# Low halves of the values: a scaled Scalar copy and a GpSimd subtraction in place of one Vector operation with a running sum

## The chip, the cores and the metric

The kernel runs on one core of a Trainium2 chip. The metric is device microseconds of one launch, the median of the runs shown. Engines are named as in the profile: PE (TensorE matmul) and PEld (its weight loads), DVE (VectorE), ACT (ScalarE), POOL (GpSimd), SP (SyncE, which issues nearly all DMAs here).

## What is computed

Top-32 attention over 4 batches and 8 heads, then a dense two-layer block with squared ReLU, then a routed layer with 8 experts. Shapes: q, k, v are 4 x 8 x 576 x 64; the dense block is 512 to 2048 to 512.

```python
scores = scale * np.matmul(q, k.transpose(0, 1, 3, 2))
kth = np.partition(scores, -top_k, axis=-1)[..., -top_k:-top_k + 1]
scores = np.where(scores >= kth, scores, -1e9)
attn = softmax(scores)                    # rows of 576, 32 kept
attn_out = np.matmul(attn, v)             # -> x, 2304 tokens x 512
...
x = np.square(np.maximum(x @ w_in, 0)) @ w_out
...
# then by token: e = argmax(x @ w_gate); out = x + gate * relu(x @ w1[e]) @ w2[e]
```

## The kernel before

Every fp32 factor that goes into a matmul is held as two fp16 numbers, a high half (the value, scaled by a power of two and rounded to fp16) and a low half (the scaled value less the high half). Products are the sum of high x high, low x high and high x low.

**The attention part** is a loop over 72 ticks `j`. A tick takes two score tiles of 128 queries x 576 keys (`a`, `b`). PE makes the scores of the next tick's tiles (`qk`, line 326), ACT copies them out of PSUM (`evac_s`, line 332), and DVE finds the 32nd largest score of each row: `tree` (line 360) takes the larger and the smaller of each pair of scores, `top32` runs four rounds of MAX8 (line 379) with MATCH_REPLACE8 between (line 382), and `mask` (line 406) compares the scores with the 32nd. ACT takes the exponential (line 401), POOL multiplies it by the mask (line 415), ACT makes the high half of the weights and their row sum (line 430), POOL the low half (line 435), and an SP DMA transposes both into `pt` (line 437). Three ticks later (`AV_LAG`) PE multiplies `pt` by the values (`av`, line 458). `e` has 3 buffers, `phl` 3, `pt` 7.

**Loads and halves of q, k and v** are "pieces". `fetch(j)` issues a piece's load into the ring `raw` of 3 buffers (line 201, an SP DMA), up to two ticks ahead; `prep(j)` makes the halves, at most three pieces a tick by its planner. For q (lines 220 to 222) and k (lines 227 to 231) ACT writes the high half, ACT scales `raw` in place, and POOL subtracts; the subtraction is put on the list `low_pool`, which is run in the middle of the next tick. For v there are 32 pieces of 128 x 320 (two heads of four pairs in four batches): ACT writes the high half into `vh[:, :, 0:D]` (line 242) and a DVE operation on the list `low_dve` makes the low half (line 245). That operation scales `raw`, subtracts the high half, writes fp16 and also sums its results along the row into one column of `v_low`; in the trace the sum is read out by a second row, DVE_READ_ACCUMULATOR. `low_dve` is run behind `top32` and ahead of the next `tree`.

**Beside the attention** run, in ticks up to 7, the conversion of the dense weights (ACT lines 278, 284, 303; DVE lines 291, 293; POOL line 304), and from tick 8 the dense block on finished tokens: PE lines 535 and 568, ACT lines 543 to 547, POOL line 556 (`gh`, the low half of the squared ReLU). After the loop come routing and the experts.

**Order.** The instructions are recorded in the order of the code and a scheduler that plans ahead with a timeline then sets the order on each engine; `tc.issue_after` keeps an instruction behind a named one. So an engine's order can change wherever a piece of work changes.

**The checks.** Near the end 128 x n tables of bounds are compared with limits (`check`, lines 1170 to 1176); if any fails, a plain path computes everything again. `v_low` is one of these tables (lines 1188 to 1190).

Of the kernel before, what the change touches and what calls it, by code (L numbers as in the profile page):

```python
# [9 lines left out]
F32 = mybir.dt.float32  # L10
# [5 lines left out]
AF = mybir.ActivationFunctionType  # L16
ALU = mybir.AluOpType
AX = mybir.AxisListType
# [3 lines left out]
B, H, S, D = 4, 8, 576, 64  # L22
# [7 lines left out]
V_EXP, W_EXP, R_EXP = 12, 8, 12  # L30
# [69 lines left out]
def attention_two_moes(ctx, tc, qm, qc, kd, vd, w_in, w_out, w_g, w1, w2, cst, out):  # L100
    nc = tc.nc
    const = ctx.enter_context(tc.tile_pool(name="const", bufs=1))
# [17 lines left out]
    nc.vector.memset(ones, 1.0)  # L120
    wgs = const.tile([128, 4, 9], F32, name="wgs")
    lg_all = const.tile([128, NT, 9], F32, name="lg_all")
    v_low = const.tile([128, 4 * H], F32, name="v_low")
    w_sq = const.tile([128, 20], F32, name="w_sq")
    w_abs = const.tile([128, 32], F32, name="w_abs")
    x_sq = const.tile([128, NT + 4], F32, name="x_sq")
# [77 lines left out]
    def new_k():  # L204
        return apool.tile([128, S], F16, name="kh", bufs=2 * BUFS["k"])

    def new_v():
        return apool.tile([128, 5, 2 * D], F16, name="vh", bufs=BUFS["v"])

    low_pool, low_dve = [], []  # L210

    def prep_piece(pc):
        vi, kind, hd, t = pc["vi"], pc["kind"], pc["hd"], pc["raw"]
        v_ = visits[vi]
        if kind[0] == "q":
            n = {"qm": 512, "ql": 256, "qc": 192}[kind]
            q = apool.tile([128, 2, n], F16, name=kind, tag=kind if kind == "qc" else "qm", bufs=BUFS[kind])
            if kind == "ql":
                t = t.rearrange("p h t -> p (h t)")
            nc.scalar.activation(q[:, 0], t, AF.Copy, scale=2.0 ** QK_EXP)  # L220
            nc.scalar.activation(t, t, AF.Copy, scale=2.0 ** QK_EXP)
            low_pool.append(lambda: nc.gpsimd.tensor_sub(q[:, 1], t, q[:, 0]))
            vq[vi, kind[:2] if kind == "qc" else "qm"] = q
        elif kind == "k":
            kh = [new_k() for _ in range(2)]
            h, l = (apool.tile([128, S], F16, name=n, bufs=2) for n in ("hp", "lp"))
            nc.scalar.activation(h, t, AF.Copy, scale=2.0 ** QK_EXP)
            nc.scalar.activation(t, t, AF.Copy, scale=2.0 ** QK_EXP)

            def finish():  # L230
                nc.gpsimd.tensor_sub(l, t, h)
                for hd in range(2):
                    for n, x in enumerate((h, l)):
                        nc.sync.dma_start(kh[hd][64 * n:64 * n + 64], x[64 * hd:64 * hd + 64])

            low_pool.append(finish)
            for hd in range(2):
                vq["k", v_["b"], v_["pr"], hd] = kh[hd]
        else:
            vh = new_v()  # L240
            t3 = t.rearrange("p (c d) -> p c d", c=5)
            nc.scalar.activation(vh[:, :, 0:D], t3, AF.Copy, scale=2.0 ** V_EXP)
            vq["v", v_["b"], v_["pr"], hd] = vh
            slot = (v_["b"] * 4 + v_["pr"]) * 2 + hd
            low_dve.append(lambda: nc.vector.scalar_tensor_tensor(
                out=vh[:, :, D:], in0=t3, scalar=2.0 ** V_EXP, in1=vh[:, :, 0:D],
                op0=ALU.mult, op1=ALU.subtract, accum_out=v_low[:, slot:slot + 1]))

    def run_all(jobs):
        while jobs:  # L250
# [86 lines left out]
    def scores(a):  # L337
        with tc.high_priority():
            qk(a)
            qk(a + 1)  # L340
            evac_s(a)
# [75 lines left out]
    def rinv(a):  # L417
        l = st[a]["pair"][2]
        nc.vector.reciprocal(l[:, 1], l[:, 0])
# [233 lines left out]
    def conv(step, j, lo, hi):  # L653
        for it in conv_at.get(j, [])[lo:hi]:
            step(*it)
# [20 lines left out]
    for j in range(NJ + AV_LAG + 1):  # L676
        a, b = 2 * j, 2 * j + 1
        live = a < NTILE
        nxt = a + 2 < NTILE
        prev = 1 <= j <= NJ  # L680
        pa, pb = a - 2, b - 2
        back = [a - 2 * AV_LAG, b - 2 * AV_LAG] if AV_LAG <= j < NJ + AV_LAG else []
        tick[0] = j
        for c in GRAM.get(j, ()):
            gram(c)
        conv(conv_split, j - 1, 2, 4)
        conv(load_w64, j, 2, 4)
        if nxt:
            scores(a + 2)
        conv(conv_act, j, 0, 2)  # L690
        step_units(HALVES / 2)
        step_units(HALVES / 2)
        conv(conv_dve, j, 0, 2)
        if live:
            if j == 0:
                tree(a)
            pair_tiles(a)
            tail = top32(a, back)
            for job in low_dve:
                with tc.issue_after(tail):  # L700
                    tail = job().ins
            low_dve.clear()
            if nxt:
                with tc.issue_after(tail):
                    tail = tree(a + 2)
            with tc.issue_after(tail):
                mask(a)
                mask(b)
        elif back:
            rinv(back[0])  # L710
        if live:
            exp_s(a)
        conv(conv_split, j, 0, 2)
        conv(conv_act, j, 2, 4)
        conv(conv_dve, j, 2, 4)
        if prev:
            apply_mask(pa)
            apply_mask(pb)
        run_all(low_pool)
        g_low()  # L720
        fetch(j)
        conv(load_w64, j + 1, 0, 2)
        if prev:
            high(pa)
            high(pb)
        x_split()
        if prev:
            low(pa)
        if live:
            exp_s(b)  # L730
        if prev:
            low(pb)
            keep_bounds(pa)
        logits()
        for i in back:
            av(i)
        for i in back:
            xout(i)
        prep(j)
        logits_turn()  # L740
# [6 lines left out]
    rpool = ctx.enter_context(tc.tile_pool(name="route", bufs=1, side="right"))  # L747
# [418 lines left out]
    good = rpool.tile([128, 9], F32, name="good")  # L1166
# [3 lines left out]
    def check(n, x, limit, op):  # L1170
        t = test[:, :x.shape[1]]
        if isinstance(limit, float):
            nc.vector.tensor_scalar(out=t, in0=x, scalar1=limit, scalar2=None, op0=op)  # L1173
        else:
            nc.vector.tensor_tensor(out=t, in0=x, in1=limit, op=op)
        nc.vector.tensor_reduce(out=good[:, n:n + 1], in_=t, axis=AX.X, op=ALU.min)  # L1176

    m15, m23, m31 = (bounds[:, :, n] for n in range(3))
# [6 lines left out]
    check(4, w_sq, 2.0 ** 17.5, ALU.is_le)  # L1185
    check(5, w_sq, 512.0, ALU.is_ge)
    check(6, w_abs, 2.0 ** -97, ALU.is_le)
    vl = rpool.tile([128, 4 * H], F32, name="vl")
    nc.vector.tensor_tensor(out=vl, in0=v_low, in1=v_low, op=ALU.mult)
    check(7, vl, 9216.0 ** 2, ALU.is_le)  # L1190
    check(8, m31, 2.0 ** -6, ALU.is_ge)
    nc.vector.tensor_reduce(out=good[:, 8:9], in_=good[:, 0:9], axis=AX.X, op=ALU.min)
    cnt_f = rpool.tile([128, 8], F32, name="cnt_f")
    nc.vector.tensor_copy(cnt_f, cnt)
    nc.vector.tensor_reduce(out=cnt_max, in_=cnt_f, axis=AX.X, op=ALU.max)
# [215 lines left out]
```

## Time and profile before

| what | us |
|---|---|
| median of 3 runs (lowest, highest) | 1027.3 (1023.33, 1030.25) |
| the profiled execution, own time | 1023.65 |
| its span | 1021.8 |
| DVE busy | 845.7 (83%) |
| PE busy | 779.8 (76%) |
| POOL busy | 767.4 (75%) |
| ACT busy | 759.8 (74%) |

The profile is one execution. Between the first and the last instruction lie 1021.8 us; the own time is 1.85 us longer. A busy share over the whole span mixes stages: the attention loop fills the first 745 us, the experts the last 250, and each has its own limit. So the views below are read by stretch. A row of a group gives an operation's busy time and mean duration, and how long its engine sat idle just before it.

### The profile page before, as it was taken

How to read it: one execution, taken by the hardware profiler on the slowest of the kernel's cores; microseconds unless marked ns; L12 is line 12 of the kernel's file. 1: busy time of each engine (PE TensorE's matmuls, PEld its weight loads, DVE VectorE, ACT ScalarE, POOL GpSimd, SP SyncE). 2: the span in 40 equal slices, each digit the busy share in tenths (PEclk: the TensorE clock that was granted, in tenths of full speed). 3: DMA queues.
4: the chain of work that ended last, by engine and by line, in shares of the span. 5: the costliest groups of instructions: out<-in, count | busy, mean ns of one | idle time of the engine just before them, and what ended most of it. 6: DMA issues, size and time to landing. Idle time of an engine off the chain costs nothing. (4 is left out here: it accounts for less than half of the span.)

```text
span 1021.8 us, 25759 instructions
## 1 busy us (share of the span) xinstructions
PE 779.8 (76%) x9036; PEld 592.5 (58%) x9036; DVE 845.7 (83%) x2279; ACT 759.8 (74%) x2117; POOL 767.4 (75%) x783
## 2 busy tenths in 40 slices
PE   0123337989879979989969999999997958688852
PEld 0122226767667757667657777767775746565631
DVE  4999999999999999999989999999908634535631
ACT  7777676899988998888779989999866642544620
POOL 4576777899879898888879988899955875744850
PEclk9999999999999999999979999999998978898876
DMA  9675554668675475565475676565537508653500
GB/s 286 174 189 152 141 126 78 103 137 156 118 161 111 94 150 94 108 130 119 100 137 121 138 138 130 116 117 90 96 64 269 208 27 326 214 177 113 177 15 10
DMA packets 257023, 138.16 MB, mean 135 GB/s; under 512 B 215348, under 2 KB 238260, under 8 KB 256848
## 3 DMA queue, kind: packets, MB, share of 16 engines
q1 hardware_dynamic: 253568, 132.16, 55.7%
q0 software_dynamic: 3280, 3.80, 1.2%
q8 instruction: 94, 1.54, 0.6%
q14 instruction: 81, 0.66, 0.2%
HBM read 76.92 MB, written 7.37 MB: 82 GB/s over the span
## 5 line engine op out<-in xcount | busy, mean ns | idle before, releaser
L379 DVE MAX8 m<-tr 128x8 f32<-128x288 f32 (+1 forms) x576 | 275.8, 517 | 0.0
L435 POOL TENSOR_TENSOR phl<-e,phl 128x576 f16<-128x576 f32 x144 | 190.6, 1328 | 33.2 <-ACT phl L430 29.0
L415 POOL TENSOR_TENSOR e<-e,mk 128x576 f32<-128x576 f32 x144 | 196.0, 1371 | 21.9 <-DVE mk L406 21.9
L568 PE MATMUL px<-woh,gh 128*128 128x512 f16 x576 | 189.3, 382 | 15.9 <-POOL gh L556 10.8
L382 DVE MATCH_REPLACE8 tr<-m,tr 128x288 f32<-128x288 f32 x432 | 186.8, 437 | 0.0
L535 PEld LDWEIGHTS <-wih 128*128 128x128 f16 x2048 | 143.2, 101 | 55.4 <-issue 23.6
L535 PE MATMUL ph<-xb,wih 128*128 128x128 f16 (+1 forms) x1792 | 156.6, 231 | 21.0 <-DMA xb<-xhl 9.5
L458 PE MATMUL misc<-vh,pt 128*128 128x64 f16 (+1 forms) x2400 | 119.3, 198 | 63.7 <-ACT xn L476 33.7
L556 POOL TENSOR_TENSOR gh<-g,gh 128x128 f16<-128x128 f32 (+1 forms) x256 | 130.2, 515 | 41.1 <-ACT gh L547 27.4
L458 PEld LDWEIGHTS <-pt 128*128 128x128 f16 (+1 forms) x2400 | 100.8, 100 | 85.3 <-issue 53.2
L568 PEld LDWEIGHTS <-gh 128*128 128x128 f16 x864 | 77.5, 100 | 86.0 <-POOL gh L556 21.1
L360 DVE SCALAR_TENSOR_TENSOR tr<-pS,s 128x576 f32<-128x576 f32 x144 | 102.1, 750 | 14.8 <-ACT s L332 10.8
L401 ACT ACTIVATE e<-s,nm 128x576 f32<-128x576 f32 x144 | 111.0, 772 | 1.4 <-POOL phl L435 0.7
L568 PE MATMUL px<-wol,gh 128*128 128x512 f16 x288 | 109.7, 382 | 0.0
L430 ACT ACTIVATE phl<-e 128x577 f16<-128x577 f32 x144 | 98.0, 681 | 2.8 <-POOL e L415 2.8
L543 ACT ACTIVATE r<-ph 128x128 f32<-128x128 f32 (+1 forms) x256 | 70.3, 287 | 37.9 <-PE ph L535 36.8
L535 PE MATMUL ph<-xb,wil 128*128 128x128 f16 (+1 forms) x896 | 97.4, 230 | 0.0
L326 PE MATMUL pS<-kh,ql 128*128 128x192 f16 x576 | 67.2, 273 | 38.9 <-DMA kh<-lp 26.1
L406 DVE TENSOR_SCALAR mk<-s,m 128x576 f16<-128x576 f32 x144 | 93.3, 688 | 0.0
L545 ACT ACTIVATE g<-r 128x128 f32<-128x128 f32 (+1 forms) x256 | 82.7, 324 | 7.1 <-POOL gh L556 3.4
L332 ACT ACTIVATE s<-pS 128x1152 f32<-128x1152 f32 x72 | 80.3, 1116 | 3.7 <-PE pS L326 3.4
L547 ACT ACTIVATE gh<-r 128x128 f16<-128x128 f32 (+1 forms) x256 | 80.7, 320 | 1.3 <-PE px L568 1.0
(229 smaller groups left out, 1585.6 us busy)
## 6 DMA issues: line engine op xcount, KB each, us to landing
wraw<-in_w SPq DMA_DIRECT2D x64, 512.0 KB, 5.4
wol<-in_w_in SPq DMA_DIRECT2D x16, 512.0 KB, 4.9
raw<-in_qm SPq DMA_DIRECT2D x48, 128.0 KB, 2.8
w<-in_w_out SPq DMA_DIRECT2D x10, 512.0 KB, 3.7
raw<-in_vd SPq DMA_DIRECT2D x32, 160.0 KB, 2.8
raw<-in_kd SPq DMA_DIRECT2D x16, 288.0 KB, 3.5
out<-x SPq DMA_DIRECT2D x16, 256.0 KB, 2.6
wol<-in_w_out SPq DMA_DIRECT2D x6, 512.0 KB, 3.7
```

The source lines that it names most:

```text
L360: last = nc.vector.scalar_tensor_tensor(out=R2[:, :, n * 288:n * 288 + 288].rearrange("p k (c x) -> p k c x", c=3), in0=near, scalar=2.0 * ...
L379: return both(lambda k: nc.vector.max(m[k][:, 8 * r:8 * r + 8], x[k][:, :n]))
L382: both(lambda k: nc.vector.match_replace(out=dst[k][:, :n], in_to_replace=m[k][:, 8 * r:8 * r + 8], in_values=src[k][:, :n], imm_value=NEG))
L401: nc.scalar.activation(e[:, :S], st[i]["s"], AF.Exp, scale=0.125, bias=st[i]["nm"])
L406: nc.vector.tensor_scalar(out=t, in0=st[i]["s"], scalar1=st[i]["m"][:, 31:32], scalar2=None, op0=ALU.is_ge)
L415: nc.gpsimd.tensor_mul(e[:, :S], e[:, :S], st[i]["mk"])
L430: nc.scalar.activation(h[:, 0, :S + 1], st[i]["e"], AF.Copy, accum_out=st[i]["l"][:, 0:1])
L435: nc.gpsimd.tensor_sub(h[:, 1, :S], st[i]["e"][:, :S], h[:, 0, :S])
L458: nc.tensor.matmul(ps[:, a, :], lhsT=pt[:rows, 5 * low + c, :], rhs=vh[:rows, c, part * D:(part + 1) * D], start=(n == 0), stop=(n == len( ...
L535: nc.tensor.matmul(ph, lhsT=wt[:, d, u["f"] * 128:(u["f"] + 1) * 128], rhs=x[:, :, c0 + d, :], start=(n == 0), stop=(n == 11))
L556: g_last[0] = nc.gpsimd.tensor_sub(u["gh"][:, 1], u["g"], u["gh"][:, 0]).ins
L568: nc.tensor.matmul(px, lhsT=gh[:, part, t * 128:(t + 1) * 128], rhs=w[:, f, :], start=(f == 0 and n == 0), stop=(f == 15 and n == 2))
```

## The change

```diff
-    v_low = const.tile([128, 4 * H], F32, name="v_low")
...
-    low_pool, low_dve = [], []
+    low_pool = []
...
             nc.scalar.activation(vh[:, :, 0:D], t3, AF.Copy, scale=2.0 ** V_EXP)
             vq["v", v_["b"], v_["pr"], hd] = vh
-            slot = (v_["b"] * 4 + v_["pr"]) * 2 + hd
-            low_dve.append(lambda: nc.vector.scalar_tensor_tensor(
-                out=vh[:, :, D:], in0=t3, scalar=2.0 ** V_EXP, in1=vh[:, :, 0:D],
-                op0=ALU.mult, op1=ALU.subtract, accum_out=v_low[:, slot:slot + 1]))
+            nc.scalar.activation(t, t, AF.Copy, scale=2.0 ** V_EXP)
+            low_pool.append(lambda: nc.gpsimd.tensor_sub(vh[:, :, D:], t3, vh[:, :, 0:D]))
...
             tail = top32(a, back)
-            for job in low_dve:
-                with tc.issue_after(tail):
-                    tail = job().ins
-            low_dve.clear()
...
-    vl = rpool.tile([128, 4 * H], F32, name="vl")
-    nc.vector.tensor_tensor(out=vl, in0=v_low, in1=v_low, op=ALU.mult)
-    check(7, vl, 9216.0 ** 2, ALU.is_le)
-    check(8, m31, 2.0 ** -6, ALU.is_ge)
-    nc.vector.tensor_reduce(out=good[:, 8:9], in_=good[:, 0:9], axis=AX.X, op=ALU.min)
+    check(7, m31, 2.0 ** -6, ALU.is_ge)
+    nc.vector.tensor_reduce(out=good[:, 8:9], in_=good[:, 0:8], axis=AX.X, op=ALU.min)
```

The values now take the path of q and k: two ACT copies and a POOL subtraction. The sum, its table and its check are gone. In the changed kernel line numbers are lower by 1 to 3 in the loop (`tree` is L357 there, `mask` L403, the mask multiplication L412, the low half of the weights L432); the new rows are L243 on ACT and L244 on POOL.

The scheduler moves other rows too. Three places show what stands around the new and the removed rows. The first is DVE, in the third batch, one tick with a value piece. Before (`m_6519` is the 32 best of the tile pair):

```order
L379 MAX m_6519<-tr 128x8 x2
L419 RECIPROCAL l<-l 128x2
L382 MATCH_REPLACE tr<-m_6519,tr 128x288 x2
L379 MAX m_6519<-tr 128x8 x2
L245 SCALAR_TENSOR_TENSOR vh,v_low<-raw,vh 128x5x64
L360 SCALAR_TENSOR_TENSOR tr<-pS,s 128x2x288 x2
L406 TENSOR_SCALAR mk<-s,m_6519 128x576 x2
```

With the change, in the same batch:

```order
L376 MAX m_6534<-tr 128x8 x2
L416 RECIPROCAL l<-l 128x2
L379 MATCH_REPLACE tr<-m_6534,tr 128x288 x2
L376 MAX m_6534<-tr 128x8 x2
L357 SCALAR_TENSOR_TENSOR tr<-pS,s 128x2x288 x2
L403 TENSOR_SCALAR mk<-s,m_6534 128x576 x2
```

The value row between the last MAX and the next tree is gone; the rest of the tick's DVE chain stands in the same order.

The second place is ACT, in the same batch (`s` is the copy of the next scores, `nm` the row maximum for the exponential, `r`, `g`, `gh` the dense block). Before:

```order
L387 ACTIVATE nm<-m_6519 128x2
L332 ACTIVATE s<-pS 128x1152
L401 ACTIVATE e_94<-s,nm 128x576
L430 ACTIVATE phl_98,l<-e_92 128x577
L543 ACTIVATE r<-ph 128x128 x2
L430 ACTIVATE phl_99,l<-e_93 128x577
L242 ACTIVATE vh<-raw 128x5x64
L545 ACTIVATE g<-r 128x128
L547 ACTIVATE gh<-r 128x128
L476 ACTIVATE xn<-misc,l 128x64 x2
```

With the change:

```order
L384 ACTIVATE nm<-m_6534 128x2
L329 ACTIVATE s<-pS 128x1152
L398 ACTIVATE e_93<-s,nm 128x576
L540 ACTIVATE r<-ph 128x128
L241 ACTIVATE vh<-raw 128x5x64
L427 ACTIVATE phl_97,l<-e_91 128x577
L542 ACTIVATE g<-r 128x128
L544 ACTIVATE gh<-r 128x128
L243 ACTIVATE raw<-raw 128x320
L473 ACTIVATE xn<-misc,l 128x64 x2
```

The new scaling row stands a few rows behind the high half, both behind the copy of the scores and ahead of the next tick's.

The third place is POOL, in the same batch (`e` by mask, `phl` the low half of the weights, `lp` the low half of k). Before:

```order
L435 TENSOR_TENSOR phl_100<-e_94,phl_100 128x576
L231 TENSOR_TENSOR lp<-raw,hp 128x576
L435 TENSOR_TENSOR phl_98<-e_92,phl_98 128x576
L556 TENSOR_TENSOR gh<-g,gh 128x128 x2
L415 TENSOR_TENSOR e_93<-e_93,mk 128x576
L556 TENSOR_TENSOR gh<-g,gh 128x128
L415 TENSOR_TENSOR e_94<-e_94,mk 128x576
```

With the change, two value rows stand within one tick:

```order
L412 TENSOR_TENSOR e_91<-e_91,mk 128x576
L553 TENSOR_TENSOR gh<-g,gh 128x128
L244 TENSOR_TENSOR vh<-raw,vh 128x5x64
L432 TENSOR_TENSOR phl_99<-e_93,phl_99 128x576
L553 TENSOR_TENSOR gh<-g,gh 128x128
L432 TENSOR_TENSOR phl_97<-e_91,phl_97 128x576
L553 TENSOR_TENSOR gh<-g,gh 128x128
L244 TENSOR_TENSOR vh<-raw,vh 128x5x64
L553 TENSOR_TENSOR gh<-g,gh 128x128
L412 TENSOR_TENSOR e_92<-e_92,mk 128x576
```

Each value subtraction stands directly ahead of a low half of the weights or shortly ahead of a mask multiplication, in the one queue of POOL.

## Rows read from the trace of the kernel before

**Rows 1.** The page: span, and each engine's busy time over it.

```profile
span 1021.8 us, 25759 instructions
PE 779.8 (76%) x9036; PEld 592.5 (58%) x9036; DVE 845.7 (83%) x2279; ACT 759.8 (74%) x2117; POOL 767.4 (75%) x783
```

**Rows 2.** Stretches: us, PE, PEld, DVE, ACT, POOL busy (count), clock, DMA share, GB/s.

```profile
0.00:152.00 152.00, 37.75 (x319) 28.25 (x319) 136.02 (x277) 111.62 (x242) 100.95 (x85) 1.00 0.65 179
152.00:745.00 593.00, 536.69 (x6602) 412.63 (x6603) 578.52 (x1696) 520.32 (x1591) 513.37 (x562) 0.97 0.63 119
240.00:268.00 28.00, 25.53 (x316) 18.74 (x314) 27.79 (x83) 26.68 (x83) 26.42 (x32) 1.00 0.82 151
250.00:310.00 60.00, 51.40 (x660) 39.60 (x658) 59.79 (x176) 54.52 (x175) 51.51 (x59) 0.97 0.68 137
434.00:508.00 74.00, 68.54 (x670) 49.79 (x669) 72.74 (x206) 60.64 (x174) 61.35 (x61) 0.95 0.60 117
555.00:592.00 37.00, 36.96 (x422) 28.46 (x420) 36.58 (x108) 33.88 (x91) 35.12 (x37) 1.00 0.69 136
592.00:656.00 64.00, 59.31 (x789) 46.33 (x788) 63.54 (x185) 57.47 (x186) 52.84 (x61) 0.97 0.66 132
```

**Rows 3.** Waits of DVE, 75 to 760 us: waiter, releaser, us, times, longest.

```profile
DVE tr L360 <- ACT s L332: 5.1, 3, 3.4
DVE l L419 <- ACT phl L430: 3.8, 1, 3.8
DVE sq L518 <- PE ph L515: 1.2, 1, 1.2
```

**Rows 4.** Lines by source: count, shortest/median/longest ns, first and last start.

```profile
L245 DVE SCALAR_TENSOR_TENSOR vh<-raw,vh x32: 461/483/1434, 63.7 to 650.6; 128x320 f16<-128x320 f32 x32
L293 DVE SCALAR_TENSOR_TENSOR wm<-wm,wr x32: 666/874/1762, 10.4 to 150.8; 128x512 int32<-128x512 int32 x32
L406 DVE TENSOR_SCALAR mk<-s,m x144: 500/592/1536, 34.2 to 740.0; 128x576 f16<-128x576 f32 x144
```

**Rows 5.** DVE groups, 0 to 152 us: count, busy us, mean ns, idle before.

```profile
L293 DVE SCALAR_TENSOR_TENSOR wm<-wm,wr 128x512 int32<-128x512 int32 x32 | 32.1, 1007 | 0.4
L291 DVE SCALAR_TENSOR_TENSOR wr<-wol,wr 128x512 int32<-128x512 int32 x22 | 22.0, 1001 | 9.1 <-ACT wr L278 9.0
...
L291 DVE SCALAR_TENSOR_TENSOR wr<-w,wr 128x512 int32<-128x512 int32 x10 | 12.4, 1241 | 0.0
...
L245 DVE SCALAR_TENSOR_TENSOR vh<-raw,vh 128x320 f16<-128x320 f32 x8 | 4.5, 594 | 0.0
```

**Rows 6.** DVE groups, 152 to 745 us.

```profile
L406 DVE TENSOR_SCALAR mk<-s,m 128x576 f16<-128x576 f32 x130 | 83.0, 678 | 0.0
...
L245 DVE SCALAR_TENSOR_TENSOR vh<-raw,vh 128x320 f16<-128x320 f32 x24 | 16.7, 706 | 0.0
```

**Rows 7.** Timeline of DVE, 118 to 121 us: start us, us, row.

```profile
118.24 0.47 DVE L245 SCALAR_TENSOR_TENSOR vh<-raw,vh 128x320 f16<-128x320 f32 x1
...
118.64 1.43 DVE L245 SCALAR_TENSOR_TENSOR vh<-raw,vh 128x320 f16<-128x320 f32 x1
...
120.00 0.68 DVE L291 SCALAR_TENSOR_TENSOR wr<-w,wr 128x512 int32<-128x512 int32 x1
```

**Rows 8.** Timeline of POOL at the same place.

```profile
118.50 1.22 POOL L304 TENSOR_TENSOR wol<-wm,woh 128x512 f16<-128x512 f32 x1 [0.33 <-ACT woh L303]
```

**Rows 9.** Timeline of ACT, 489 to 494 us.

```profile
489.94 0.47 ACT L242 ACTIVATE vh<-raw 128x320 f16<-128x320 f32 x1 [3.63 <-DMA raw<-in_vd]
490.32 0.19 ACT L387 ACTIVATE nm<-m 128x2 f32<-128x2 f32 x1
```

**Rows 10.** Line 222, POOL's subtractions for q: shortest/median/longest ns.

```profile
L222 POOL TENSOR_TENSOR ql<-raw,ql x48: 662/676/1243, 5.6 to 713.4; 128x256 f16<-128x256 f32 x48
...
L222 POOL TENSOR_TENSOR qm<-raw,qm x8: 1153/1161/1372, 316.0 to 444.7; 128x512 f16<-128x512 f32 x8
```

**Rows 11.** Waits of ACT, 75 to 760 us.

```profile
ACT vh L242 <- DMA raw<-in_vd: 15.2, 15, 3.6
```

## Prediction

> **What bounds the kernel now.** I read the page first: DVE is the busiest engine, but 83% over the span says little, since the stages differ [rows 1]. So next the stretches. From 152 to 745 us DVE is busy 578.52 of 593 us, 98%, while ACT has 520.32 (88%), POOL 513.37 (87%) and PE 536.69 [rows 2]. Then the waits of DVE: from 75 to 760 us it waits for others 10.1 us in all, in five places [rows 3]. So in the attention loop DVE sets the pace: a DVE row less is time won, as long as nobody else becomes later than DVE. The reader should see the second half of that sentence too: POOL and ACT have only 12 to 13% left, and the work that leaves DVE goes to exactly these two.
>
> **What is removed.** 32 DVE rows of line 245, from 63.7 to 650.6 us, at 461 to 1434 ns [rows 4]. A row's duration overlaps the next row's start: the one at 118.24 is 0.47 long and the next starts at 118.64, 0.40 later [rows 7]. So I take 0.07 off each; the read-out of the sum adds nothing to that, as the next row starts with it. Eight lie before 152 us at a mean of 594 ns [rows 5], 24 later at 706 ns [rows 6]: 8 x 0.524 = 4.2 us and 24 x 0.636 = 15.3 us, 19.5 us of DVE's chain. All of them stand between the last MAX and the next tree, where DVE does not wait, so all of it is on the path.
>
> Part of that is waiting and not work. The row at 118.64 took 1.43 us, about 0.96 more than its neighbour, while a POOL subtraction ran from 118.50 to 119.72 [rows 7, 8]. The Trainium skill says why (SBUF — State Buffer, section on SBUF's two separate sides): VectorE with two SBUF inputs and GpSimd share a port pair as an exclusive lock, and whoever comes second waits for the whole instruction; this trace agrees with 0.96 us here.
>
> The square of `v_low` and its check near 765 us are a few small rows; I cost them at nothing, under 1 us, and leave them out.
>
> **What DVE pays back.** The work comes back as 32 POOL subtractions, and POOL rows hold up DVE rows. In the first 152 us lines 291 and 293 take 341 (32 times), 335 (22) and 575 ns (10) above the shortest row of 666 [rows 4, 5]: 10.9 + 7.4 + 5.8 = 24.1 us for 100.95 us of POOL [rows 2], 0.24 us for each us of POOL. Later only the masks do: 130 x (678 - 500) = 23.1 us for 513.37 us of POOL [rows 2, 4, 6], 0.045 per us.
>
> A subtraction of 128x320 isn't in the trace. POOL's 128x256 has a median of 676 ns, its 128x512 1161 [rows 10]: on that line 320 columns take 0.80 us. The bounds are 0.80 and the longest 128x256 row, 1.24; I take 0.85, a little above the line, since most rows lie near the median. Early that costs DVE 8 x 0.85 x 0.24 = 1.6 us, later 24 x 0.85 x 0.045 = 0.9 us. Left for DVE: 2.6 us early, 14.4 us later, 17.0 in all. This is the ceiling.
>
> **What ACT and POOL can take.** The added ACT copy has the shape of line 242, which holds ACT from 489.94 to 490.32, 0.38 us [rows 9]: 32 x 0.38 = 12.2 us, 9.1 of them after 152 us. POOL gets 20.4 us after 152 us. On average both fit: POOL would have 533.8 us in a stretch of some 579. But the value pieces come in bursts. The three stretches with the 24 later rows are 250:310, 434:508 and 592:656, 198 us together. There POOL has 51.51 + 61.35 + 52.84 = 165.7 us, ACT 54.52 + 60.64 + 57.47 = 172.6 [rows 2]. With the new rows POOL has 186.1, ACT 181.7. How full can they be while DVE keeps going? At 555:592 POOL is busy 35.12 of 37 (95%) with DVE at 99%; at 240:268 ACT has 26.68 of 28 (95%), DVE again 99% [rows 2]. At 95% POOL needs 186.1 / 0.949 = 196 us for these stretches, so they would shrink by 2 us only; 250:310 alone would need 61.4. ACT needs 181.7 / 0.953 = 191, so 7 us. How much of POOL's work may slide into the ticks between? A value's low half is needed three ticks later, and `gh` has four buffers; against it, `raw` has three, and `e` three: a late low half of the weights holds back the exponential. So the later gain lies between 2 and 14.4 us. I take 7: what ACT's share allows, and near the middle of POOL's two ends.
>
> Early there is room: in the first 152 us ACT has 111.62 and POOL 100.95 [rows 2], and the new rows are 3.0 and 6.8 us. The 2.6 us stand.
>
> **Moved loads.** A `raw` buffer was freed by DVE behind the last MAX; now it is freed by POOL, behind whatever POOL has queued. The next load on SP waits for it, and the transposes of the weights are queued behind that load. ACT already waits for value loads 15 times, 15.2 us in all [rows 11]. I cost the delay at nothing, since loads are issued up to two ticks ahead; without that cover, one more us for each of 24 pieces on ACT would use up ACT's 7 us and 17 more. That is in the rivals.
>
> **Sum.** 1023.65 (the profiled execution's own time) - 2.6 - 7 = 1014.1 us. The median of the runs is 1027.3, 3.65 above that execution, so on the median's scale 1027.3 - 9.6 = 1017.7; I say 1018.
>
> **Rivals.**
> 1. *DVE's ceiling is reached.* POOL and ACT let their work slide and every removed row counts: 1027.3 - 17.0 = 1010.3. For it: POOL at 95% and ACT at 95% with DVE at 99% [rows 2]. Against it: 250:310 would have POOL above 95%.
> 2. *POOL takes DVE's place in the bursts.* Then the later gain is 2 us, or, if each subtraction stands in line ahead of a mask multiplication and nothing slides, a loss of 24 x (0.85 - 0.636) = 5.1 us: 1027.3 - 2.6 - 2 = 1022.7 to 1027.3 - 2.6 + 5.1 = 1029.8, middle 1026. For it: the order of POOL, where the new rows stand directly ahead of low halves of the weights. The Trainium skill's warning is of this kind (Perfetto Trace Analysis, section on optimizing Scalar and DVE operations): moving work from a saturated VectorE to GpSimd might not help, as the two share an SBUF port; by it alone the later gain would be none, and the 0.045 us per us above says that the lock alone is too small for that here.
> 3. *Slower.* The new rows run at their contended price, 1.24 us, with no cover, because the exponential waits for one of three `e` buffers behind them: 24 x (1.24 - 0.636) = 14.5, less 2.6, so 1039. It decides from the point where a piece costs the chain 0.54 us more than before, 24 x 0.54 = 10.3 + 2.6. Late `raw` loads would end there too. Against it: the shortest and the median row are 14 ns apart, so most POOL rows aren't contended [rows 10], and ACT has 12% to spare.
> 4. *The change doesn't do what it says*, since the scheduler orders all engines anew: DVE's 10.1 us of waits could be gone or be twice as long. This has no sign; it widens every case by some 5 us.
>
> **How the numbers follow.** A measurement of this kernel can tell about 1% from no change: below 1017.0 is faster, above 1037.6 slower. Partial gain (1018) 0.45, ceiling (1010) 0.25, POOL the bound (1026) 0.20, slower (1039) 0.10. My forecast lies on the edge: of its 0.45 I give 0.17 to faster and 0.28 to the same. Faster 0.25 + 0.17 = 0.42, same 0.28 + 0.20 = 0.48, slower 0.10. The range reaches from the ceiling less some 3 us of re-ordering, 1007, to just above rival 2's far end, 1031; the slower case and a little on either side are left out.
>
> **What would show it.** In the new profile no line 245 on DVE; 32 rows on POOL near 0.85 us and 32 on ACT near 0.47 as a row. If I am right, the loop ends some 9 us earlier, DVE stays above 96% busy from 152 us on, and in the three bursts POOL stands at 92 to 96%. Rival 1 shows DVE at 98% there and POOL's work spread past the bursts. Rival 2 shows the tree or the reciprocal waiting for ACT, ACT waiting for POOL's low halves, and DVE at 92% or less in the bursts. Rival 3 shows long waits of ACT for value loads or of SP for POOL's value rows. What would make me wrong most: a subtraction of 320 columns that takes over 1 us, or a re-ordering that moves DVE's own waits by 10 us.

## The result and the profile after

The median went from 1027.26 us (1023.33 to 1030.25, four runs) to 1010.46 us (1008.54 to 1015.88, four runs). The ratio is 0.9857 [0.9819, 0.9896]: faster by 1.4%, 16.8 us. A second set, in which both kernels ran again unchanged, gave 1024.86 and 1008.47, ratio 0.9858 [0.9811, 0.9904]. The forecast was 1018; the result lies inside the range, and near rival 1, the ceiling of 1010.3. By the prediction's own line of 1017.0 it is faster, to which it gave 0.42, against 0.48 for no change.

The profiled execution took 1011.29 us, 12.4 less than that of before (1023.65). Its page, against [rows 1]:

```profile
span 1009.4 us, 25811 instructions
PE 775.6 (77%) x9036; PEld 590.3 (58%) x9036; DVE 832.4 (82%) x2212; ACT 769.9 (76%) x2149; POOL 790.1 (78%) x815
```

DVE has 13.3 us less to do, POOL 22.7 us more, ACT 10.1 us more. Where the span became shorter is seen from the phases. Each phase begins and ends with a row: the attention loop ends with DVE's last mask row (line 406, 403 in the changed kernel); the stretch behind it ends with the first routing row on DVE (`ent`, line 768, now 761); the routing ends with the first weight load for the experts' matmuls on PEld (line 1042, now 1035); the experts end with the first check row behind their last matmul (`good` on DVE, line 1176, now 1169).

| us | before | after | before again | after again |
|---|---|---|---|---|
| loop ends at | 740.7 | 725.6 | 739.5 | 721.2 |
| stretch to the routing | 24.0 | 32.5 | 24.2 | 32.4 |
| routing | 76.9 | 76.5 | 77.2 | 74.5 |
| experts | 164.6 | 159.3 | 162.6 | 159.2 |
| tail | 15.5 | 15.5 | 17.6 | 16.8 |
| span | 1021.8 | 1009.4 | 1021.0 | 1004.1 |

The "last 250 us" that stand above as the experts' hold the routing too. The loop gained 15.1 us (18.3 in the second pair), the stretch behind it gave 8.5 us (8.2) back, and the experts gained 5.3 us (3.4); the routing gained 0.4 (2.7).

The stretches of the loop, first of before and then of after; columns as in [rows 2]:

```profile
0.00:740.70 740.70, 570.14 (x6859) 437.61 (x6860) 714.37 (x1971) 628.37 (x1820) 610.02 (x643) 0.98 0.63 131
```

```profile
0.00:725.60 725.60, 558.81 (x6752) 431.93 (x6753) 699.72 (x1907) 633.38 (x1835) 632.69 (x670) 0.98 0.64 133
245.00:300.00 55.00, 46.54 (x599) 35.55 (x596) 54.37 (x154) 52.69 (x164) 53.87 (x63) 0.97 0.65 139
418.00:490.00 72.00, 63.36 (x712) 48.21 (x711) 71.27 (x200) 63.76 (x190) 65.55 (x71) 1.00 0.61 110
575.00:638.00 63.00, 56.01 (x742) 44.48 (x741) 62.27 (x179) 59.73 (x183) 58.67 (x66) 0.95 0.66 136
```

DVE's busy time fell by 14.65 us, and the loop by 15.1: DVE's idle time, 740.70 - 714.37 = 26.3 before and 25.9 after, stayed. So POOL and ACT did not make DVE wait more. In the first burst POOL is busy 53.87 of 55 us, 98%, and DVE 54.37, 99%: the 95% that the prediction took for POOL's limit is none. The other two bursts have POOL at 91 and 93%.

The new rows, by source: count, shortest/median/longest ns, first and last start; against [rows 4]:

```profile
L244 POOL TENSOR_TENSOR vh<-raw,vh x32: 783/794/1351, 42.0 to 621.9; 128x320 f16<-128x320 f32 x32
L243 ACT ACTIVATE raw<-raw x32: 452/464/536, 37.0 to 618.6; 128x320 f32<-128x320 f32 x32
L403 DVE TENSOR_SCALAR mk<-s,m x144: 499/675/1625, 35.7 to 725.0; 128x576 f16<-128x576 f32 x144
```

The subtraction has a mean of 0.867 us (0.85 was taken), the copy a median of 464 ns. The median mask row rose from 592 to 675 ns; the mean rose from 688 to 711, 144 x 0.023 = 3.3 us (from 683 to 697 in the second pair, 2.1). The groups of the two pages, before and after:

```profile
L406 DVE TENSOR_SCALAR mk<-s,m 128x576 f16<-128x576 f32 x144 | 93.3, 688 | 0.0
```

```profile
L403 DVE TENSOR_SCALAR mk<-s,m 128x576 f16<-128x576 f32 x144 | 96.8, 711 | 0.0
```

POOL's queue shows how the burst was spread. In the timeline of POOL between 376 and 456 us stand all eight subtractions of the middle burst, three of them here; before, the eight DVE rows stood between 435 and 503 us.

```profile
377.15 0.79 POOL L244 TENSOR_TENSOR vh<-raw,vh 128x320 f16<-128x320 f32 x1
396.65 0.79 POOL L244 TENSOR_TENSOR vh<-raw,vh 128x320 f16<-128x320 f32 x1
...
443.47 0.80 POOL L244 TENSOR_TENSOR vh<-raw,vh 128x320 f16<-128x320 f32 x1 [1.28 <-ACT raw L243]
```

So the subtractions were not put off into later ticks: they came earlier. The high halves of this burst, on ACT, start from 371.0 to 450.9 us where they started from 380.8 to 489.9, and over all 32 pieces a low half starts 5 us behind its high half (median; 2.5 to 7.4), where it was 13 (5.5 to 54.6). A `raw` buffer is free that much sooner.

The waits of DVE to 760 us, in the form of [rows 3] (which begin at 75 us):

```profile
DVE ent L761 <- PE px L565: 29.0, 1, 29.0
DVE wr L288 <- ACT wr L275: 11.1, 3, 9.4
DVE tr L357 <- ACT s L329: 6.6, 3, 3.6
DVE l L416 <- ACT phl L427: 3.3, 1, 3.3
```

Inside the loop there is no new wait. The long one, 29.0 us, is the stretch behind the loop. It ends with `ent`, a copy that needs memory which the attention part has held. The view names a matmul of the dense block, which ended at about that moment; in the kernel before it names a transfer, the last transpose of the attention's output. That transpose is what both wait for: SP's issue of it and the row `ent`, first before, then after:

```profile
761.43 1.23 SPq L500 DMA_TRANSPOSE xb<-xhl  x1
764.72 0.45 DVE L768 CAST ent<-cs 128x18 int32<-128x18 f32 x1 [20.07 <-DMA xb<-xhl]
```

```profile
754.76 1.27 SPq L497 DMA_TRANSPOSE xb<-xhl  x1
758.10 0.45 DVE L761 CAST ent<-cs 128x18 int32<-128x18 f32 x1 [29.00 <-PE px L565]
```

In all 14 profiles `ent` starts 3.2 to 3.3 us behind that issue, whatever the view names. The transpose needs the halves of the attention's output, and these need PE's last product of weights and values (`av`). It starts 12.5 us behind the last mask before and 20.9 after: 8.4 of the 8.5 us. So the question is what PE does ahead of it. First before, then after:

```profile
740.00:765.00 25.00, 25.00 (x314) 18.88 (x312) 1.13 (x7) 16.52 (x64) 13.62 (x25) 1.00 0.39 67
```

```profile
725.00:758.00 33.00, 33.00 (x404) 24.27 (x403) 0.81 (x3) 21.29 (x81) 15.39 (x28) 1.00 0.34 62
```

PE is busy all the time in both, at a granted clock of 1.00 (2.4 GHz). How much was left for it is read from what it had done by the end of the loop. The groups of PE up to that point, by line, of before and of after (`px`: second products of the dense block; `ph`: first ones):

```profile
L568 PE MATMUL px<-woh,gh 128*128 128x512 f16 x478 | 157.6, 381 | 13.4 <-POOL gh L556 8.4 <-ACT gh L547 4.6
L535 PE MATMUL ph<-xb,wih 128*128 128x128 f16 (+1 forms) x1441 | 129.0, 233 | 20.2 <-DMA xb<-xhl 9.5 <-ACT r L543 8.5 <-ACT x2t L600 1.4
L568 PE MATMUL px<-wol,gh 128*128 128x512 f16 x240 | 91.3, 381 | 0.0
L535 PE MATMUL ph<-xb,wil 128*128 128x128 f16 (+1 forms) x720 | 79.8, 232 | 0.0
```

```profile
L565 PE MATMUL px<-woh,gh 128*128 128x512 f16 x468 | 154.1, 382 | 22.7 <-POOL gh L553 15.8 <-ACT gh L544 6.6
L532 PE MATMUL ph<-xb,wih 128*128 128x128 f16 (+1 forms) x1400 | 124.0, 231 | 11.7 <-ACT r L540 8.9 <-DMA xb<-xhl 1.9 <-ACT x2t L597 0.6
L565 PE MATMUL px<-wol,gh 128*128 128x512 f16 x234 | 88.9, 380 | 0.0
L532 PE MATMUL ph<-xb,wil 128*128 128x128 f16 (+1 forms) x700 | 75.7, 230 | 0.0
```

By the end of the loop 16 `px` and 61 `ph` fewer are done, and 30 of the 64-column products of the attention. Started one behind the other they stand 0.216, 0.056 and 0.029 us apart in the trace: 3.5 + 3.4 + 0.9 = 7.8 us. PE takes its matmuls in the order of its list: between the last mask and the last `av` stand 19 `px`, 84 `ph` and 60 products of the attention before, and 36, 144 and 90 after; behind it the same are left in both (127 and 126 `px`, 444 `ph`), and they run beside the routing. So PE has some 8 us more to do ahead of the last `av`, and the stretch is 8.5 us longer.

### The profile page after: what moved, and what is told of

The parts are those of the page before. It is cut to its first block, busy times and chain, and to the rows that moved or that the text cites. A ratio compares the mean times of both kernels' runs of the same rounds, so it can differ in the third digit from the quotient of the medians.

```text
span 1009.4 us, 25811 instructions
## 1 busy us (share of the span) xinstructions
PE 775.6 (77%) x9036; PEld 590.3 (58%) x9036; DVE 832.4 (82%) x2212; ACT 769.9 (76%) x2149; POOL 790.1 (78%) x815
## 5 line engine op out<-in xcount | busy, mean ns | idle before, releaser
L412 POOL TENSOR_TENSOR e<-e,mk 128x576 f32<-128x576 f32 x144 | 197.6, 1384 | 15.2 <-DVE mk L403 13.6
L432 POOL TENSOR_TENSOR phl<-e,phl 128x576 f16<-128x576 f32 x144 | 187.9, 1311 | 24.1 <-ACT phl L427 20.8
L553 POOL TENSOR_TENSOR gh<-g,gh 128x128 f16<-128x128 f32 (+1 forms) x256 | 127.6, 507 | 38.2 <-ACT gh L544 24.8
L455 PE MATMUL misc<-vh,pt 128*128 128x64 f16 (+1 forms) x2400 | 121.5, 198 | 34.5 <-ACT xn L473 20.2
L455 PEld LDWEIGHTS <-pt 128*128 128x128 f16 (+1 forms) x2400 | 101.2, 100 | 64.2 <-issue 27.7
L357 DVE SCALAR_TENSOR_TENSOR tr<-pS,s 128x576 f32<-128x576 f32 x144 | 102.3, 751 | 13.3 <-ACT s L329 6.6
L403 DVE TENSOR_SCALAR mk<-s,m 128x576 f16<-128x576 f32 x144 | 96.8, 711 | 0.0
L532 PE MATMUL ph<-xb,wil 128*128 128x128 f16 (+1 forms) x896 | 95.3, 229 | 0.0
L540 ACT ACTIVATE r<-ph 128x128 f32<-128x128 f32 (+1 forms) x256 | 69.8, 287 | 26.9 <-PE ph L532 25.6
L323 PEld LDWEIGHTS <-ql 128*128 128x128 f16 x576 | 55.3, 110 | 56.0 <-ACT wr L275 21.5
```

What stands on the lines that cost most here:

```text
L323: nc.tensor.matmul(ps[:, c], lhsT=q[:, part], rhs=kh[:, c * 192:(c + 1) * 192], start=(n == 0), stop=(n == 2 * len(jobs) - 1))
L357: last = nc.vector.scalar_tensor_tensor(out=R2[:, :, n * 288:n * 288 + 288].rearrange("p k (c x) -> p k c x", c=3), in0=near, scalar=2.0 * ...
L412: nc.gpsimd.tensor_mul(e[:, :S], e[:, :S], st[i]["mk"])
L432: nc.gpsimd.tensor_sub(h[:, 1, :S], st[i]["e"][:, :S], h[:, 0, :S])
L455: nc.tensor.matmul(ps[:, a, :], lhsT=pt[:rows, 5 * low + c, :], rhs=vh[:rows, c, part * D:(part + 1) * D], start=(n == 0), stop=(n == len( ...
L532: nc.tensor.matmul(ph, lhsT=wt[:, d, u["f"] * 128:(u["f"] + 1) * 128], rhs=x[:, :, c0 + d, :], start=(n == 0), stop=(n == 11))
```

## The experiments

All times stand beside the kernel before on the same chip, which took 1024.86 to 1026.15 us in these sets.

**The pair again (e5, e6).** Both kernels without an edit.

> The changed kernel once more, for a second profile. In the first two profiles the loop ended 15.1 us earlier, the stretch from there to routing was 8.5 us longer, routing 0.5 and the experts 5.3 us shorter. Theory A, the loop and the stretch behind it belong to the change and the experts' 5.3 us to the execution: loop end 724 to 728, stretch 30 to 35, experts anywhere from 159 to 165. Rival, the experts are shorter because of the change: 158 to 160 again. Time 1008 to 1015.

> The kernel before once more, for a second profile. Theory A: loop end 739 to 742, the stretch behind it 23 to 25, experts anywhere from 159 to 165. Rival, the experts were longer before: 163 to 166 again. Time 1022 to 1030.

Measured: 1008.47 and 1023.45 (ratios to before 0.9858 [0.9811, 0.9904] and 0.9983 [0.9959, 1.0007]). The phases stand in the table above. What repeats within 0.2 us is the stretch behind the loop, and within some 3 us each the gains of the loop, of the routing and of the experts. The loop of the changed kernel ended at 721.2, earlier than the 724 to 728 that was expected, so one kernel's loop moves by 4.4 us from one execution to another.

**DVE's rows twice (e1).** The kernel before, with each low half computed twice.

```diff
             for job in low_dve:
-                with tc.issue_after(tail):
-                    tail = job().ins
+                for _ in range(2):
+                    with tc.issue_after(tail):
+                        tail = job().ins
```

> The kernel before with each of the 32 DVE rows of the values' low half issued twice (the second writes the same numbers). Theory A, the removed DVE rows stood on the chain that sets the loop: 32 more rows cost what 32 fewer were reckoned at, 8 x 0.52 + 24 x 0.64 = 19.5 us in the loop, some of it taken back by a shorter stretch between the loop and routing (the change lengthened that stretch by 8.5 us in its profile): 1038 to 1047 against 1027 for the kernel before. Rival B, the gain came from the new order of all engines and not from the rows: within 5 us of 1027.

Measured: 1038.63, ratio 1.0103 [1.0071, 1.0135]. The loop ends at 765.0 against 740.7, 24.3 us later, with 23.8 us more of DVE: 0.74 us for each of the 32 rows, where 0.61 (19.5 / 32) was reckoned. DVE's rows are on the path, fully. The stretch behind the loop is 19.0 instead of 24.0: it took 5 us of the loss back, where it had taken from the gain.

**Without the running sum (e2).** The DVE operation stays, its sum and the check on it go.

```diff
             low_dve.append(lambda: nc.vector.scalar_tensor_tensor(
                 out=vh[:, :, D:], in0=t3, scalar=2.0 ** V_EXP, in1=vh[:, :, 0:D],
-                op0=ALU.mult, op1=ALU.subtract, accum_out=v_low[:, slot:slot + 1]))
+                op0=ALU.mult, op1=ALU.subtract))
```

> The kernel before with the DVE operation kept, but without its running sum, the table v_low and its check. Theory A, the sum is free (the next row starts with the read-out row) and the gain came from moving the operation: 1022 to 1030. Rival, the sum itself held DVE up: below 1018.

Measured: 1022.73, ratio 0.9968 [0.9928, 1.0009]; the loop ends 3.8 us earlier. The rows, by source:

```profile
L243 DVE SCALAR_TENSOR_TENSOR vh<-raw,vh x32: 465/480/1521, 62.6 to 647.2; 128x320 f16<-128x320 f32 x32
```

A median of 480 ns against 483 with the sum [rows 4]: no cost of the sum can be measured, and the gain of the change isn't from here: the 3.8 us are no more than two executions of one kernel differ by, and the interval of the ratio holds 1.

**POOL's subtractions twice (e4).** The changed kernel, each subtraction done two times.

```diff
-            low_pool.append(lambda: nc.gpsimd.tensor_sub(vh[:, :, D:], t3, vh[:, :, 0:D]))
+            for _ in range(2):
+                low_pool.append(lambda: nc.gpsimd.tensor_sub(vh[:, :, D:], t3, vh[:, :, 0:D]))
```

> The changed kernel with each of the 32 POOL subtractions issued twice: 32 x 0.87 = 28 us more POOL. Theory A, POOL still has room and the work slides: 1010 to 1016 (2.5 us of hold-up on DVE, and a little). Rival, POOL stands at its edge (53.9 of 55 us busy in the first burst after the change): each of the three bursts grows by 3 to 6 us, 1019 to 1028.

Measured: 1036.36, ratio to before 1.0096 [1.006, 1.0132]; 26 us more than the changed kernel, above both expectations. The loop ends at 744.4, 18.8 us later, for 25.6 us more of POOL in it (658.3 against 632.7). Of the 18.8 us, 12.8 are more DVE work and 5.9 more DVE idle time. The rest lies behind the loop, where no subtraction runs (stretch 34.9 against 32.5, experts 163.8 against 159.3). Its longest wait of DVE, its masks in DVE's groups, and a stretch of it:

```profile
DVE tr L358 <- ACT s L330: 14.9, 6, 7.7
```

```profile
L404 DVE TENSOR_SCALAR mk<-s,m 128x576 f16<-128x576 f32 x144 | 108.4, 787 | 0.0
```

```profile
418.00:500.00 82.00, 72.61 (x790) 53.96 (x788) 81.06 (x221) 72.44 (x212) 78.00 (x86) 0.99 0.59 114
```

This is rival 2 as it looks when it comes: the tree waits for ACT six times, 14.9 us, the longest 7.7, POOL stands at 95% over a whole burst, and the masks take longer (a mean of 787 ns against 711, 144 x 0.076 = 11 us). So the change's subtractions, 27.7 us of POOL, cost the loop nothing that shows, and the next 25.6 us lengthen it by 18.8. Whether POOL is the bound is not told by its busy share alone: 78.00 of 82 here with DVE waiting, 53.87 of 55 in the changed kernel without.

**Without the subtraction (e3, e7).** Two kernels of the changed one with POOL's part taken out, ACT writing the low half in place of the scaled copy.

```diff
-            nc.scalar.activation(t, t, AF.Copy, scale=2.0 ** V_EXP)
-            low_pool.append(lambda: nc.gpsimd.tensor_sub(vh[:, :, D:], t3, vh[:, :, 0:D]))
+            nc.scalar.activation(vh[:, :, D:], t3, AF.Copy, scale=2.0 ** V_EXP)   # e3
+            nc.scalar.activation(vh[:, :, D:], t3, AF.Copy, scale=0.0)             # e7
```

> The changed kernel without the 32 POOL subtractions: ACT writes the second half of the values straight from raw (the high half once more, so the low half is left out of the result); ACT's work is that of the changed kernel. Theory A, POOL took the subtractions nearly free: only the reckoned hold-up of DVE comes back, 1.6 + 0.9 = 2.5 us, so 1005 to 1011 against 1010. Rival, POOL is at its edge in the three bursts and eats a part of the gain: 1003 or less (the 4 us by which the bursts fell short of DVE's ceiling, and the hold-up).

> The changed kernel without the 32 POOL subtractions; ACT writes zeros into the second half instead of scaling raw, so its row count and sizes are those of the changed kernel, and the low half of the values is left out of the result. Theory A, POOL takes the subtractions nearly free at this load: within 5 us of the changed kernel, 1005 to 1016. Rival, POOL eats part of the gain: 1003 or less.

Measured: the first took 5114.89, which can't be compared: with the high half counted twice the program's own bounds sent it down its plain path, which computes everything again. Only its loop counts, and that ends at 729.4. The second took 1019.04, ratio 0.9947 [0.9921, 0.9974], its loop ending at 726.8. With POOL relieved of 26 us the loop is no shorter than in the changed kernel (725.6 and 721.2), and one mask row takes 0.717 and 0.705 us, no less than 0.711 and 0.697. No cost of the subtractions shows in the loop, on POOL or by holding up masks. But e7 missed both expectations of its time: with less work it is 9 to 11 us slower than the changed kernel. Its stretch behind the loop is 36.1 against 32.5 us, and its profiled execution, 1014.6, was the fastest of its ten runs; what the rest of its median is, no row shows. The scheduler orders every engine anew for each kernel; in the stretch this is seen (40 `px` and 171 `ph` ahead of the last `av`, against 36 and 144), for the rest it is a guess.

**PE relieved (e9, e10).** Both kernels with the third of the dense block's three first products left out, so that PE has less work behind the loop.

```diff
-        for wt, c0 in ((wih, 0), (wih, 4), (wil, 0)):
+        for wt, c0 in ((wih, 0), (wih, 4)):
...
-                                 start=(n == 0), stop=(n == 11))
+                                 start=(n == 0), stop=(n == 7))
```

> The kernel before with the third product of the dense block's first layer (low half of w_in times high half of x) left out: 1024 of its 3072 matmuls, about 57 us of PE at 0.056 each, are gone; the low half of w_in is so left out of the result. Control for the next run. Theory A (DVE sets the loop, PE the stretch behind it): loop end 735 to 743 as before, the stretch behind it shorter than 24 by several us, time 1010 to 1024. Rival (PE holds the loop too): loop end below 733.

> The changed kernel with the same 1024 PE matmuls left out. Theory A, half of the loop's 16.7 us is given back since PE has to finish the dense block behind the loop (32.5 us against 24.1): with less for PE the stretch behind the loop comes out within 3 us of that of the run before it, and the two light kernels differ by 17 to 24 us in time. Rival, the longer stretch has another cause (the order of the last ticks, the last tokens' transposes): the stretches differ by 6 us or more again, and the times by 12 to 18 us.

Measured: 1013.41 and 1012.0, ratios to before 0.9871 [0.9846, 0.9895] and 0.9866 [0.9825, 0.9908]. By their profiles:

| us | before, light | after, light |
|---|---|---|
| loop ends at | 741.7 | 731.0 |
| stretch to the routing | 18.9 | 19.5 |
| routing | 74.6 | 74.7 |
| experts | 165.4 | 168.9 |
| span | 1015.8 | 1009.2 |

The stretch does what was expected: relieved of PE's work it differs by 0.6 us between the two kernels, not by 8.5. The last `av` starts 12.0 and 11.4 us behind the last mask, where it was 12.5 and 20.9. So the give-back is PE's backlog ahead of it. The view names the transfer in both, first in the relieved kernel of before, then of after:

```profile
DVE ent L768 <- DMA xb<-xhl: 15.1, 1, 15.1
```

```profile
DVE ent L761 <- DMA xb<-xhl: 15.7, 1, 15.7
```

The time does not do what was expected: without the give-back the pair should have differed by 17 to 24 us, and it differs by 6.6 in the profiles and by 1.4 in the medians, which is no difference. In the profiles the loop gains 10.7 instead of 15 to 18 (after, a mask row takes 0.749 us, before 0.709; 5.8 us over 144), and the experts lose 3.5. The execution profiled for before was the slowest of its four, 1017.65. What makes the medians agree stays open.

**The tick's fill (e8).** The changed kernel with more units of the dense block asked for in each tick.

```diff
-HALVES = 4.4
+HALVES = 4.8
```

> The changed kernel with 4.8 in place of 4.4 units of the dense block per tick. The stretch behind the loop is PE finishing the dense block; it grew from 24.0 to 32.5 us since the ticks got shorter and the units per tick did not change. Theory A, that is where 8.5 us were given back, and more units per tick get them: stretch 20 to 27 us, loop within 3 us of 726, 1001 to 1007. Rival, ACT and POOL are so full that more units per tick lengthen the loop by as much: 1008 to 1016.

Measured: 1011.86, ratio 0.9879 [0.9847, 0.991]; loop 724.2, stretch 35.4. By tick 20, 40 and the end of the loop PE had issued 49, 131 and 269 us of dense products (at 0.216 and 0.056 each), in the changed kernel 48, 127 and 269. The loop ends where theory A had it, but the stretch misses its 20 to 27: the larger number is asked for in the ticks behind the last mask too, and 48 `px` and 216 `ph` now stand ahead of the last `av`. The number asked for is not what holds PE back in the loop, and the give-back can't be had again in this way.

**ACT's copy twice (e11).** The changed kernel, with the high half written two times.

```diff
-            nc.scalar.activation(vh[:, :, 0:D], t3, AF.Copy, scale=2.0 ** V_EXP)
+            for _ in range(2):
+                nc.scalar.activation(vh[:, :, 0:D], t3, AF.Copy, scale=2.0 ** V_EXP)
```

> The changed kernel with the high half of the values written twice by ACT: 32 x 0.38 = 12.2 us more ACT. Theory A, ACT still has room in the loop (634 of 723 us): 1006 to 1014 against 1009. Rival, ACT stands at its edge in the bursts as POOL does: 1017 or more.

Measured: 1013.87, ratio 0.9884 [0.9864, 0.9905]. Its loop as a stretch:

```profile
0.00:725.30 725.30, 562.38 (x6692) 431.88 (x6693) 695.94 (x1907) 641.52 (x1858) 631.40 (x667) 0.94 0.63 134
```

The loop ends at the same place (725.3), with ACT's busy time 8.1 us higher; the stretch behind the loop is 3.6 us longer. So ACT has room for the copy and for another of its size, by the loop's end. Inside it the tree waits for ACT 11.5 us, against 6.6 in the changed kernel and 10.8 in the one before, once for 5.1 us right behind the first burst:

```profile
DVE tr L358 <- ACT s L330: 11.5, 4, 5.1
```

This is made up by masks that are shorter here, 686 against 711 ns on the mean, 3.6 us. Whether the second copy or the new order makes the longer wait is not shown. For the single copy of the change ACT's share, on which the 7 us of the forecast rested, did not limit the gain.

**Half of the change (e12).** Without the sum, the heads alternating between DVE and the new way.

```diff
+            if hd:
+                low_dve.append(lambda: nc.vector.scalar_tensor_tensor(...))
+            else:
                 nc.scalar.activation(t, t, AF.Copy, scale=2.0 ** V_EXP)
                 low_pool.append(lambda: nc.gpsimd.tensor_sub(vh[:, :, D:], t3, vh[:, :, 0:D]))
```

> Half the change: of each pair of heads one low half by ACT and POOL as in the changed kernel, the other by DVE as before, without the running sum. Theory A, the DVE rows are the price and each counts alike: the loop ends about half of 16.7 us earlier than before, 730 to 734, and the time is 1013 to 1021. Rival, POOL at its edge eats the later half of the gain: loop end 722 to 728, time 1011 or less.

Measured: 1022.08, ratio 0.9973 [0.9945, 1.0001]. The loop ends at 734.8, 5.3 us earlier than the 740.1 of the two profiles of before, where the whole change brings 15 to 18: a third, not a half. The stretch behind it is 26.5. Of 5.3 us 2.4 are given back. Both expectations are missed, of the loop by little and of the time by more. By DVE's rows, each counted to the start of the next, the value rows fell from 19.5 to 10.5 us, about half as they should; the masks took 1.9 us more, the MAX rows 1.1 and line 293's rows 1.2. No version beat the changed kernel.

## Why the prediction was right, and where it was not

**What bounds the loop: right.** DVE sets the pace. Doubling its rows lengthened the loop by what DVE's busy time rose (24.3 and 23.8 us), and the change shortened it by what DVE's fell (15.1 and 14.65). In 12 of the 14 profiles DVE is idle for 23.3 to 27.0 us of the loop, so the loop is DVE's work and a constant; the other two are those with more work on ACT (29.4, e11) and on POOL (31.8, e4).

**What is removed: right.** 19.5 us were reckoned. In the two profiles of before the value rows hold DVE, from each one's start to the next row's, for 19.5 and 21.4 us. Counted in the same way the masks came back with 3.4 and 2.1 us, the MAX rows with 1.8 and 1.7 and the two rows of `x_sq` with 1.3, while lines 291 and 293 took 1.6 and 2.9 less: together the 14.6 and 19.1 by which DVE's work fell. The loop gained 15.1 and 18.3, the mean 16.7; the reckoned ceiling, after what DVE pays back, was 17.0. What a second copy of the row costs, 0.74 (e1), is more than the row itself, 0.61 and 0.67.

**Early gain: 3.5 and 4.9 us against 2.6.** So far the trees of the changed kernel moved forward from the first tick to tick 19, in the two pairs. The pay-back of 1.6 us, reckoned from POOL's rows and DVE's rows of lines 291 and 293, did not show: those rows kept their length or became shorter (line 293, now 290, has a mean of 988 ns against 1007; line 291, now 288, 1009 and 1134 against 1001 and 1241).

**Late gain: the step that failed.** The forecast took 7 us out of 14.4, by a limit of 95% on ACT and POOL in the three bursts. The trees gained 3.4, 3.6 and 3.4 us over the three, 10.4 together (13.9 in the second pair). POOL went to 98% in the first, and its subtractions of the second stood up to 58 us ahead of the DVE rows that they replace; the forecast had asked only how far they might slide to later. The rows on which the 95% rested [rows 2] showed stretches in which POOL and ACT happened to be that full; none showed DVE waiting for them at that level. A busy share that an engine reached while nobody waited is a floor for what it can do, not a cap. The edge is there, though: the next 25.6 us on POOL lengthened the loop by 18.8 (e4).

**What DVE pays back by POOL's rows: right in size, by other rows.** 0.9 us late was reckoned; 3.3 and 2.1 was the masks' rise in all. But without any subtraction the masks are as long (e3, e7), so it isn't the added POOL work that does it here. The trace shows what does: when the two engines meet. In the changed kernel 39 of the 144 masks start while no POOL row runs and take 514 ns on the mean; the other 105 take 784. Before it was 61 at 524 and 83 at 808. So more masks met a POOL row, but only one of them met a value subtraction (two in the second profile); in e4 ten did. Of the 78 masks over 0.9 us in the first profile of before and the two of after, 77 end 0.31 to 0.32 us behind the end of a POOL row. The Trainium skill's exclusive lock (SBUF — State Buffer, section on SBUF's two separate sides), by which the one that comes second waits for the whole instruction, agrees with this.

**Moved loads at nothing: right, and better than that.** The fear was that POOL would free `raw` later. It was freed sooner, 5 us behind the high half where it had been 13, and ACT waited for value loads 5.9 us in four places, against 15.2 us in 15 [rows 11].

```profile
ACT vh L241 <- DMA raw<-in_vd: 5.9, 4, 3.0
```

**Not in the sum: the stretch behind the loop, +8.5 us.** The prediction carried the loop's gain straight to the end. PE, which nothing in the sum named, has its dense block spread over the loop, and what it has not done by the last mask and has on its list ahead of the last `av` stands between loop and routing: 7.8 us more after the change. That this is where the gain went is shown: relieved of PE's work, the stretch no longer differs (18.9 and 19.5). That the shorter loop alone puts it there is not: with the longer loop of e1 the stretch shrinks by 5 us, as it should, but the loop of e4 is 3.7 us longer than that of before and its stretch is 34.9. The order that the scheduler plans for each kernel, or the load on POOL and ACT, which feed the dense block, may have a part in it; how large a part stays open.

**Not in the sum: the experts, -5.3 and -3.4 us.** Their instructions are the same. One wait of PE for a transfer of expert weights is shorter, first before and then after:

```profile
PE ph L1042 <- DMA wraw<-in_w: 5.4, 1, 5.4
```

```profile
PE ph L1035 <- DMA wraw<-in_w: 2.5, 1, 2.5
```

That would be 2.9 us of the 5.3; in the second pair the wait is 6.7 and 2.9, 3.8 us where the phase gained 3.4. Over all kernels here the phase took 159 to 169 us, without a pattern that follows the change (168.9 in e10, which has it), so why it is shorter stays open.

**The net.** Loop -15.1, stretch +8.5, routing -0.4, experts -5.3: -12.3 of the 12.4 in the profiles, where -9.6 was predicted; in the second pair -18.3, +8.2, -2.7 and -3.4, 16.9 with the tail. In the loop rival 1 is what happened. The forecast's total came near by luck: its loop gain was 5.5 to 8.7 us too small, and it missed a give-back of 8 and a gain of 3 to 5 behind it. That the median of 1010.46 falls on rival 1's 1010.3 is luck as well, for the same two terms were missing there. Rival 2 did not come true at this load, and did in part with twice the subtractions (e4). The Trainium skill warns (Perfetto Trace Analysis, section on optimizing Scalar and DVE operations) that moving work between VectorE and GpSimd might not help; here it did (ratio 0.9857), and with twice the subtractions it did not (1.0096). Rival 3's waits of ACT did not show. Rival 4, the new order, was taken at some 5 us; e7, slower by 9 to 11 us with less work, may be more of it, which is not shown.

## What to carry to other kernels

Work moved off the pacing engine was won here although the engines that took it were 89 to 98% busy in the bursts; it stood earlier than before. So look at where the moved work may stand, and not only at the busy share of the stretch where it stood. Follow the gain past the end of the loop: an engine whose work fills the loop's gaps may leave more of it undone, and what stands ahead of the last result that is needed is paid for behind. A wait can be put down to a row that merely ended at the same time, so see whether the same distance to another event holds in every run. Two versions whose order a scheduler plans anew differed by a per cent here without a cause that could be found (e7), so test a mechanism by its place in the trace as well as by the total.

## What the runs showed of the hardware

POOL was busy 53.87 of 55 us while DVE was busy 54.37: both can be full at once on rows like these. A subtraction of 128x320 took a median of 794 ns on POOL, between the 676 of 128x256 and the 1161 of 128x512 [rows 10]. The running sum of the DVE operation cost nothing that can be measured: the shortest row took 465 ns without it and 461 with it. And removing all of the subtractions from POOL left the masks on DVE as long as they were (0.717 and 0.705 us against 0.711 and 0.697): a mask that starts while no POOL row runs took 514 ns, one that starts beside one 784, so the price depends on when the two meet and not only on how much POOL does.
